# Blockwise causal attention and a gated MLP on one core: Q and K loads of four heads, a third xq buffer, and a looser rule for early fillers

## The chip, the cores and the metric

The kernel runs on one core of a Trainium2 chip. The metric is device time in microseconds of one execution. TensorE is written PE, VectorE DVE, ScalarE ACT, GpSimd POOL and SyncE SP, as the profile does.

## The reference

There are 8 batches of 8 heads, 576 positions and 64 values per head. Attention is causal by blocks of 64 positions; its output, 4608 rows of 512, goes through a two-layer network with a gate.

```
scores = q @ k.T / sqrt(64);  masked where block(row) < block(column), block = position // 64
attn   = exp(scores - max) / sum;   x = (attn @ v) as [4608, 512]
h = x @ w_in                       # [512, 2048]
g = h / (1 + exp(-beta * h))
out = g @ w_out                    # [2048, 512], float32
```

## The kernel before

**Units.** Attention works in 32 units of one batch and two heads (`u = 4 * b + c`). In a unit PE multiplies Q and K (L692; repeats with held weights appear as L434), ACT takes the exponential of 1024 columns at a time into `E` (L706, and L718 for the last 64), DVE clears the masked blocks with memsets (L712, L714), PE multiplies by V with a column of ones added for the sums (L744, 30 matmuls for five query tiles and two heads), and DVE takes the reciprocal (L756) and writes the normalised output to `xq` (L763), a tile of bf16 of which there are two. `xq` is then turned into `xT`: by PE and a copy in batches 0 to 2 (L783, L791 or L793), by a DMA transpose that SP issues in batches 3 to 7 (L770, `XB = 3`). A unit's P·V takes an `xq` slot when it is placed, and the slot is free again when its transpose has read it.

**Loading Q and K.** In batches 0 and 1 each unit loads its own two heads of Q and of K (L606), casts them (L613, POOL or DVE), and PE turns them (L622) into `QKT` through a DVE copy (L630). From batch 2 on (`QB = 2`) one load takes all eight heads of Q, another all eight of K (L641), each into one of two staging tiles `ST` of 128 x 36 x 64 float32 (the slots of class `S8`; the six small parts `ST6` of batches 0 and 1 are cut from the same memory). POOL casts them per two heads into `QKn` (L653, eight casts a batch), and one DMA transpose for two units makes `QKT` (L660). V comes in six loads a batch (L536, L539), and POOL casts it per two heads (L562).

**MLP.** Its rows are cut into nine chunks of 512. For each, PE makes 16 tiles of h (L955), ACT a tanh (L965), and DVE the gated product `gT` (L969). Chunk 0 is multiplied by `w_out` plainly (L991); chunks 1 to 8 use a seven-product scheme for 2 x 2 blocks with sums made on DVE (L852, products L885, evacuation L900 and L903). Weights are loaded by POOL's queue (L490 for `w_in`, L495 for `w_out`).

**What sets the order.** A planner, `Plan.schedule`, simulates five engines, two DMA rings, eight PSUM banks and all buffer slots with durations that are written into the kernel. It gives each engine a fixed list of instructions, and semaphore waits follow from the dependencies. Engines then work through their lists in order. Where a tile takes a slot or a bank, its users are made to depend on the last users of that slot or bank.

Loads of Q, K and V are chained in one order (`seq`, each with `after` the one before), and those behind the first 30 are lazy: they are placed only when the planner has less than 3 us of transfers left in SP's ring. In the order, V of a batch follows the loads of Q and K of unit `4 * b + 1` (from batch 2 on).

**Fillers.** Up to 400 small matmuls with no use for the result (L511 in whole form, L513 as a pair on two halves of the array) are offered to the planner at the lowest priority until 50 us of its time. One is placed where PE has nothing else and enough of banks 4 to 7 are free:

```
if o.fill and (now > o.fill or sum(k >= 4 for k in banks) < 3):
    continue
```

A filler takes one of these banks for 110 ns of the plan, and like every user it waits for the bank's last users.

Of the kernel before, what the change touches and what calls it, by code (L numbers as in the profile page):

```python
# [7 lines left out]
bf16 = mybir.dt.bfloat16  # L8
# [3 lines left out]
NPAIR = 4  # L12
# [36 lines left out]
class Plan:  # L49
# [8 lines left out]
    FIRST, LAND0, BOTH0 = 14000.0, 2150, .8  # L58
    BACKLOG = 3000.0
    RING = 6000.0  # L60

    def __init__(self):
        self.ops = []
# [19 lines left out]
    def schedule(self):  # L83
        free = {c: list(range(n)) for c, n in self.classes.items()}
        last = {(c, i): [] for c, n in self.classes.items() for i in range(n)}
        banks = list(range(8))
# [15 lines left out]
        now, nsched = 0.0, 0  # L102
# [66 lines left out]
        while nsched < len(self.ops) - len(fill) or pend or rings["H"] or rings["S"] or late:  # L169
            if not events:  # L170
                raise RuntimeError("the plan has no way on")
            now = heapq.heappop(events)
            flow(now)
            while pend and pend[0][0] <= now + 1e-9:
                _, _, o = heapq.heappop(pend)
# [20 lines left out]
            while progress:  # L196
                progress = False
                for e in engs:
# [4 lines left out]
                    for o in pool:  # L203
                        if e not in o.engs:
                            continue
                        if o.ready + o.rest + slack > now + 1e-9:
                            heapq.heappush(events, o.ready + o.rest + slack)
                            continue
                        if o.after is not None and o.after.start is None:
                            continue  # L210
                        if o.lazy and left["H"] > self.BACKLOG:
                            continue
                        if o.fill and (now > o.fill or sum(k >= 4 for k in banks) < 3):
                            continue
                        if not can(o):
                            continue
                        if len(o.engs) > 1:
                            other = [x for x in o.engs if x != e]
                            if any(eng_free[x] <= now and len([1 for q in pool if x in q.engs and q.ready <= now]) <
                                   len([1 for q in pool if e in q.engs and q.ready <= now]) for x in other):  # L220
                                continue
                        if o.fill:
                            o.mode = mode or "full"
                        k = (o.prio, o.idx) if e in ("PE",) else (o.prio, o.ready, o.idx)
                        if e == "PE" and mode is not None and o.mode != mode:
                            k = (o.prio + 0.25, o.idx)
                        if best is None or k < best[0]:
                            best = (k, o)
                    if best is None:
                        continue  # L230
                    o = best[1]
                    pool.remove(o)
                    for t in o.tiles:
                        if t.slot is None:
                            if t.cls == "PP":
                                a = next(a for a in t.at if a in banks and a + 1 in banks)
# [24 lines left out]
                    if o.dma is not None:  # L261
                        x = "S" if e == "POOL" else "H"
# [92 lines left out]
def bass_blockwise_causal_attn__then__act_swish_beta_kernel(  # L355
# [10 lines left out]
    with es:  # L366
        def sb(name, shape, dt):
            return es.enter_context(nc.sbuf_tensor(name, shape, dt))

        NQ = 2  # L370
        QB, XB, CAST = 2, 3, "POOL"
        NE = 3
        PARTS = [((0, 4, "SP", range(6)), (4, 8, "SP", range(2)), (4, 8, "POOL", range(2, 6)))] + [((0, 8, "SP", range(6)),)] * 7
        GROUPS = [((0,), (1,), (2,), (3,))] + [((0, 1), (2, 3))] * 7
        NS = 6
# [2 lines left out]
        RX = 5 * RC  # L378
        OV = sb("OV", [128, 5120], f32)
        ST = [sb(f"ST{i}", [128, 36, 64], f32) for i in range(2)]  # L380
        ST6 = [s[0:96].rearrange("p t d -> p (t d)")[:, 768 * i:768 * i + 768].rearrange("p (h j d) -> p h j d", h=2, j=6)
               for s in ST for i in range(3)]
        Vs = [sb("Vs0", [128, 5, 8, 64], f32), OV[:, 2560:5120].rearrange("p (t h d) -> p t h d", t=5, h=8)]
# [3 lines left out]
        QKn = [sb(f"QKn{i}", [128, 2, 2, 768], bf16) for i in range(NQ)]  # L387
        Vn = [sb(f"Vn{i}", [128, 5, 8, 66], bf16) for i in range(NQ)]
        QKT = [sb(f"QKT{i}", [128, 2, 2, 640], bf16) for i in range(3)]
# [4 lines left out]
        E3 = [e[:, 0:3072].rearrange("p (c h n) -> p c h n", c=3, h=2) for e in Ef]  # L394
        E4 = [e[:, 3072:3136] for e in Ef]
        inv = [sb(f"inv{i}", [128, 10], f32) for i in range(3)]
        xq = [sb(f"xq{i}", [128, 5, 128], bf16) for i in range(2)]
        xT = sb("xT", [128, 4, RX], bf16)
        identF = sb("identF", [128, 128], f32)
        identB = sb("identB", [128, 128], bf16)  # L400
# [10 lines left out]
        identW = identF[:].bitcast(bf16)  # L411
        NFILL, TFILL = 400, 50000.0
        P = Plan()
        for c, n in (("ST", NS), ("QKn", NQ), ("V", NQ), ("Vs", NQ), ("QKT", 3), ("E", NE), ("EX", 1), ("inv", 3), ("xq", 2),
                     ("th", 3), ("gT", 2), ("ost", NO), ("S2", 1), ("S3", 1)):
            P.slots(c, n)
        P.slots("S8", 2)

        def mm(n):
            return max(n / 2.4 + 3, 55.0)  # L420
# [50 lines left out]
        for i in range(NQ, NE + 1):  # L471
# [4 lines left out]
                  xfer=100, dma=("d_beta", 1), prio=0.1)  # L476
# [107 lines left out]
            return [z for z in ((0, n, x0), (n, 5 - n, 0)) if z[1]]  # L584

        xt = []
        whole, early6 = {}, []
        QKI, QKX = 1000, 5400
        for u in range(NU):
            b, c = divmod(u, NPAIR)  # L590
            Tv = tl[b]
            p = c % 2
# [5 lines left out]
            if b < QB:  # L598

                turned = []  # L600
                for w, (nm, src) in enumerate((("Q", q), ("K", k))):
                    ts, pt = P.tile("ST"), P.tile("P1")
                    early6.append(ts)

                    def fl(g, e, ts=ts, src=src, b=b, c=c):
                        return [g.dma_start(ST6[ts.slot].rearrange("p h j d -> p h (j d)"),  # L606
                                            src[b, 2 * c:2 * c + 2].rearrange("h (p j) d -> p h (j d)", j=6))]

                    o = ld[nm, u] = P.op("SP", 420, fl, tiles=[ts], xfer=1170, prio=u, dma=["d_S", 0, 1])
                    o.pkt = 80.0  # L610

                    def fn(g, e, ts=ts, tn=tn, p=p, w=w):
                        return g.tensor_copy(QKn[tn.slot][0:96, p, w, :].rearrange("p (j h d) -> p j h d", j=6, h=2),  # L613
                                             ST6[ts.slot].rearrange("p h j d -> p j h d"))

                    onp = u not in (0, 3) or w == 1
                    o = P.op("POOL" if onp else "DVE", 850 if onp else 750, fn, deps=[o], tiles=[ts, tn],
                             prio=-40 + 3 * u if onp else -1)

                    def ft(g, e, tn=tn, pt=pt, p=p, w=w):  # L620
                        for i in range(6):
                            z = g.transpose(PSb[:, pt.slot, 96 * i:96 * i + 96],  # L622
                                            QKn[tn.slot][0:96, p, w, 128 * i:128 * i + 128], identB[0:96, 0:96])
                        return z

                    o = P.op("PE", 6 * 43, ft, deps=[o, c4], tiles=[tn, pt, tt_], lat=6 * 43 + 170, mode="full",
                             prio=pr(u))

                    def fc(g, e, pt=pt, td=tt_, p=p, w=w):
                        return g.tensor_copy(QKT[td.slot][:, p, w, 0:576].rearrange("c (p j) -> c p j", j=6),  # L630
                                             PSb[:, pt.slot, 0:576].rearrange("c (j p) -> c p j", j=6))

                    turned.append(P.op("DVE", dve_t(576), fc, deps=[o], tiles=[pt, tt_], prio=-5))
            elif p == 0:

                for w, (nm, src) in enumerate((("Q", q), ("K", k))):
                    if c == 0:
                        ts = whole[w] = P.tile("S8")

                        def fl(g, e, ts=ts, src=src, b=b):  # L640
                            return [g.dma_start(ST[ts.slot][:], src[b].rearrange("h t d -> (h t) d").rearrange(  # L641
                                "(i p) d -> p i d", p=128))]

                        o = P.op("SP", QKI, fl, deps=[o for t in early6 for o in t.users] if b == QB else [],
                                 tiles=[ts], xfer=QKX, prio=u, dma=["d_S8", 0, 1])
                        for i in range(NPAIR):
                            ld[nm, u + i] = o
                    ts, o = whole[w], ld[nm, u]
                    for a in range(2):
                        def fn(g, e, ts=ts, tn=tn, a=a, w=w, c=c):  # L650
                            x = ST[ts.slot][:, 9 * (c + a):9 * (c + a) + 5, :]
                            x = bass.AP(x.tensor, x.offset, [x.ap[0], [64, 5], [256, 2], [1, 64]])
                            return g.tensor_copy(  # L653
                                QKn[tn.slot][:].rearrange("p a w n -> p (a w n)")[:, 640 * (2 * a + w):][:, 0:640]
                                .rearrange("p (t h d) -> p t h d", t=5, h=2), x)

                        casts.append(P.op(CAST, 740, fn, deps=[o], tiles=[ts, tn], prio=u))

                def ft(g, e, tn=tn, td=tt_):
                    return [g.dma_start_transpose(QKT[td.slot][:].rearrange("c a w (t n) -> c (a w t) n", n=128),  # L660
                                                  QKn[tn.slot][:].rearrange("p a w n -> p (a w n)")[:, 0:2560])]

                turned = [P.op("SP", 3250, ft, deps=casts, tiles=[tt_, tn], xfer=3200, prio=-1, dma=["d_T", 0, 1])]
# [421 lines left out]
```

## Time and profile before

| | |
|---|---|
| median of 10 runs | 340.74 us (339.1 to 345.13) |
| profiled execution, its own time | 342.27 us |
| its span, first to last instruction | 340.4 us |
| PE busy, all matmuls | 324.7 us |
| ACT busy | 211.8 us |
| DVE busy | 219.1 us |
| POOL busy | 83.7 us |
| SP's hardware DMA queue | 58.3% of 16 engines' span, 39.14 MB |
| mean granted PE clock | 0.990 |

The page divides the span into 40 slices and gives each engine's busy share as a digit. A line of a wait names the waiting instruction, what released it, the total, the count and the longest. In timelines a row gives the start, the duration, the engine, the line and operation, the output and input, and in square brackets the idle time before it and its releaser. SPq is the queue of DMA instructions on SP: the duration there is that of issuing. Busy times of PE are modelled, so a busy PE is not always a PE at its peak.

### The profile page before, as it was taken

Reading aid. Unit: us, or ns where it says so; the run is one execution under the profiler, and the core shown is the slowest. Engines: PE = TensorE matmul, PEld = TensorE weight load, DVE = VectorE, ACT = ScalarE, POOL = GpSimd, SP = SyncE. Lnnn points to the kernel's source line nnn. Section 1 sums busy time; section 2 is a strip of 40 time slices with the busy share of each in tenths; the row PEclk is TensorE's granted clock in tenths of the full one; section 3 lists DMA queues with packets and bytes.
Section 4 is the critical chain, followed back from the end, with each engine's and each line's share of the span. In section 5 each row is a group of like instructions: output and inputs, shape, how many; then the busy total and the mean of one; then the engine's idle time right before and its main releaser. Section 6 shows DMA issues by size and latency. Waiting matters only on the chain.

```text
span 340.4 us, 7452 instructions
## 1 busy us (share of the span) xinstructions
PE 324.7 (95%) x3104; PEld 205.1 (60%) x3081; DVE 219.1 (64%) x447; ACT 211.8 (62%) x314; POOL 83.7 (25%) x127
## 2 busy tenths in 40 slices
PE   7798999999998999998999998999999999999995
PEld 4376446544686447754665676566656766666684
DVE  4718867479563788447966674667576766666742
ACT  1862994278636886777688736877677545544511
POOL 7675180216414300531044205303000000000000
PEclk9789999999999999999999999999999999999999
DMA  8999899999999595999879999994221211110023
GB/s 217 224 240 232 192 228 237 226 235 220 207 212 203 143 214 113 188 223 188 168 156 209 196 218 230 185 212 113 73 60 24 79 34 33 37 57 31 17 78 123
DMA packets 113313, 53.41 MB, mean 157 GB/s; under 512 B 83568, under 2 KB 112768, under 8 KB 113280
## 3 DMA queue, kind: packets, MB, share of 16 engines
q1 hardware_dynamic: 98432, 39.14, 58.3%
q10 hardware_dynamic: 9280, 9.44, 8.5%
q0 software_dynamic: 5568, 4.36, 8.1%
q8 instruction: 24, 0.39, 0.5%
q14 instruction: 9, 0.07, 0.1%
HBM read 36.71 MB, written 9.44 MB: 136 GB/s over the span
## 4 chain that ended last, share of the span: by engine, by line
PE 79%; ACT 8%; DVE 5%; DMA 4%; issue 2%; POOL 0%; POOLq 0%; ACTq 0%
PE PS L955 30%; PE PS L885 26%; PE PS L744 7%; PE PS L692 7%; DMA xT<-xq 4%; ACT E L706 4%; PE PS L991 4%; ACT th L965 3%; DVE gT L969 2%; PE PS L511 2%; PE PS L513 2%; PE PS L783 1%; PE PS L622 1%; DVE xq L763 1%; DVE QKT L630 1%
## 5 line engine op out<-in xcount | busy, mean ns | idle before, releaser
L955 PE MATMUL PS<-xT,w_in 128*128 128x512 bf16 x543 | 130.8, 379 | 4.1 <-DMA xT<-xq 1.3
L965 ACT ACTIVATE th<-PS,beta 128x512 f32<-128x512 f32 x144 | 96.7, 696 | 60.9 <-PE PS L955 60.3
L969 DVE SCALAR_TENSOR_TENSOR gT<-th,PS 128x512 f16<-128x512 f32 x144 | 95.8, 681 | 38.9 <-ACT th L965 38.1
L706 ACT ACTIVATE E<-PS 128x1024 bf16<-128x1024 f32 x93 | 92.1, 1027 | 32.3 <-PE PS L692 32.2
L955 PEld LDWEIGHTS PS<-xT,w_in 128*128 128x128 bf16 x576 | 53.0, 98 | 57.9 <-issue 2.7
L885 PE MATMUL PS<-w_out,gT 128*128 128x256 f16 x512 | 63.9, 273 | 0.3 <-ACT ost L900 0.3
L885 PEld LDWEIGHTS PS<-w_out,gT 128*128 128x128 f16 x512 | 48.7, 98 | 12.3 <-issue 0.6
L653 POOL CAST QKn<-ST 128x640 bf16<-128x640 f32 x48 | 36.2, 754 | 46.1 <-DMA ST<-in_k_dram 25.8
L562 POOL CAST Vn<-Vs 128x640 bf16<-128x640 f32 (+1 forms) x28 | 21.2, 755 | 94.1 <-DMA Vs<-in_v_dram 92.9
L692 PE MATMUL PS<-QKT 64*64 64x64 bf16 (+4 forms) x328 | 37.7, 302 | 0.4 <-ACT E L706 0.3
L744 PEld LDWEIGHTS PS<-Vn,E 128*128 128x128 bf16 x930 | 31.3, 97 | 7.3 <-DVE E L712 2.4
L744 PE MATMUL PS<-Vn,E 128*128 128x65 bf16 x930 | 32.6, 193 | 2.5 <-DVE E L712 1.2
L885 PE MATMUL PS<-OV 128*128 128x256 f16 x256 | 32.1, 273 | 0.0
L900 ACT ACTIVATE ost<-PS 128x512 f32<-128x512 f32 x32 | 19.2, 600 | 20.6 <-PE PS L885 20.2
L692 PEld LDWEIGHTS PS<-QKT 64*128 64x128 bf16 (+1 forms) x328 | 13.6, 96 | 26.6 <-issue 13.9
L885 PEld LDWEIGHTS PS<-OV 128*128 128x128 f16 x256 | 24.3, 98 | 5.8 <-issue 0.4
L763 DVE TENSOR_TENSOR xq<-PS,inv 128x640 bf16<-128x640 f32 x32 | 26.2, 820 | 0.7
L903 DVE SCALAR_TENSOR_TENSOR ost<-PS,ost 128x512 f32<-128x512 f32 x24 | 16.4, 688 | 13.4 <-PE PS L885 8.7
L712 DVE MEMSET E<- 64x64 uint32 x62 | 6.9, 112 | 26.3 <-ACT E L706 24.5
L852 DVE TENSOR_TENSOR OV<-gT 128x1024 f16<-128x1024 f16 x32 | 22.1, 703 | 0.4
L885 PE MATMUL PS<-OV,gT 128*128 128x256 f16 x128 | 15.9, 273 | 0.0
L991 PE MATMUL PS<-w_out,gT 128*128 128x512 f16 x64 | 15.2, 380 | 0.0
(60 smaller groups left out, 172.9 us busy)
## 6 DMA issues: line engine op xcount, KB each, us to landing
out_dram<-ost ACTq DMA_DIRECT2D x36, 256.0 KB, 2.8
Vs<-in_v_dram SPq DMA_DIRECT2D x24, 256.0 KB, 5.0
ST<-in_q_dram SPq DMA_DIRECT2D x8, 288.0 KB, 6.4
ST<-in_k_dram SPq DMA_DIRECT2D x8, 288.0 KB, 6.6
w_in<-in_moe_w_in_dram POOLq DMA_DIRECT2D x4, 512.0 KB, 10.3
w_out<-in_moe_w_out_dram POOLq DMA_DIRECT2D x4, 512.0 KB, 11.6
OV<-in_v_dram SPq DMA_DIRECT2D x4, 256.0 KB, 10.3
Vs<-in_v_dram SPq DMA_DIRECT2D x6, 128.0 KB, 7.9
```

The lines of the kernel that those rows point to most:

```text
L562: return g.tensor_copy(Vn[t.slot][:, 0:n, g0:g1, 0:64], Vs[ts.slot][:, 0:n, g0:g1, :])
L653: return g.tensor_copy(QKn[tn.slot][:].rearrange("p a w n -> p (a w n)")[:, 640 * (2 * a + w):][:, 0:640] .rearrange("p (t h d) -> p t h d ...
L692: z = g.matmul(o, QKT[tqk.slot][r, p, 1, 128 * t + y:128 * t + m + y], x)
L706: return g.activation(E3[es_(te)][:, g0, :, :], PS[:, ps.slot:ps.slot + 2, :], ACT.Exp, scale=0.125)
L744: z = g.matmul(o, eblk(te, t, i, h), Vn[Tv.slot][:, t, 2 * c + h, 0:65], start=(t == 0), stop=(t == i))
L763: return g.tensor_tensor(xq[tx.slot][:].rearrange("p i (h d) -> p h i d", h=2), both(pv, 0, 64), x, ALU.mult)
L852: return P.op("DVE", dve_t(SZ * HC / 2), mk(lambda g: g.tensor_tensor(fo(), fx(), fy(), op)), deps=deps, tiles=tiles, prio=prio)
L885: x = g.matmul(PS[:, ps.slot, HM * w:HM * w + HM], fa()[:, j, 128 * w:128 * w + 128], fb()[:, j, :], start=first and w == 0 and j == 0, st ...
L955: z = g.matmul(PS[:, ph.slot, :], w_in[:, c, 128 * j:128 * j + 128], xT[:, c, row % RX:row % RX + RC], start=(c == 0), stop=(c == 3))
L965: return g.activation(th[tt.slot][:], PS[:, ph.slot, :], ACT.Tanh, scale=beta[:, j:j + 1])
L969: return g.scalar_tensor_tensor(out=gT[tg.slot][:, j, :], in0=th[tt.slot][:], scalar=1.0, in1=PS[:, ph.slot, :], op0=ALU.add, op1=ALU.mult)
L991: z = g.matmul(PS[:, po.slot, 0:d1 - d0], gT[tg.slot][:, j, 128 * w:128 * w + 128], w_out[:, j, d0:d1], start=(j == 0), stop=(j == NJ - 1))
```

## The change

There are three parts. Fillers that are planned before 24 us need one free bank of 4 to 7 instead of three; later ones need three as before. From batch 2 on, a load brings four heads of Q or K (two units) instead of eight, into one of four half tiles `STh` that are cut from the same two staging tiles; with it the planner's figures for such a load are halved (issue 1000 to 550 ns, transfer 5400 to 2700 ns), and because the loads of Q and K are now those of units `4 * b` and `4 * b + 2`, V of a batch stands in the load order between the first and the second pair. There are three `xq` buffers instead of two.

```diff
--- before.py
+++ after.py
@@ -58,6 +58,7 @@
     FIRST, LAND0, BOTH0 = 14000.0, 2150, .8
     BACKLOG = 3000.0
     RING = 6000.0
+    EARLY = 24000.0
 
     def __init__(self):
         self.ops = []
@@ -210,7 +211,7 @@
                             continue
                         if o.lazy and left["H"] > self.BACKLOG:
                             continue
-                        if o.fill and (now > o.fill or sum(k >= 4 for k in banks) < 3):
+                        if o.fill and (now > o.fill or sum(k >= 4 for k in banks) < (3 if now > self.EARLY else 1)):
                             continue
                         if not can(o):
                             continue
@@ -378,6 +379,7 @@
         RX = 5 * RC
         OV = sb("OV", [128, 5120], f32)
         ST = [sb(f"ST{i}", [128, 36, 64], f32) for i in range(2)]
+        STh = [s[:, 18 * i:18 * i + 18] for s in ST for i in range(2)]
         ST6 = [s[0:96].rearrange("p t d -> p (t d)")[:, 768 * i:768 * i + 768].rearrange("p (h j d) -> p h j d", h=2, j=6)
                for s in ST for i in range(3)]
         Vs = [sb("Vs0", [128, 5, 8, 64], f32), OV[:, 2560:5120].rearrange("p (t h d) -> p t h d", t=5, h=8)]
@@ -394,7 +396,7 @@
         E3 = [e[:, 0:3072].rearrange("p (c h n) -> p c h n", c=3, h=2) for e in Ef]
         E4 = [e[:, 3072:3136] for e in Ef]
         inv = [sb(f"inv{i}", [128, 10], f32) for i in range(3)]
-        xq = [sb(f"xq{i}", [128, 5, 128], bf16) for i in range(2)]
+        xq = [sb(f"xq{i}", [128, 5, 128], bf16) for i in range(3)]
         xT = sb("xT", [128, 4, RX], bf16)
         identF = sb("identF", [128, 128], f32)
         identB = sb("identB", [128, 128], bf16)
@@ -411,10 +413,10 @@
         identW = identF[:].bitcast(bf16)
         NFILL, TFILL = 400, 50000.0
         P = Plan()
-        for c, n in (("ST", NS), ("QKn", NQ), ("V", NQ), ("Vs", NQ), ("QKT", 3), ("E", NE), ("EX", 1), ("inv", 3), ("xq", 2),
+        for c, n in (("ST", NS), ("QKn", NQ), ("V", NQ), ("Vs", NQ), ("QKT", 3), ("E", NE), ("EX", 1), ("inv", 3), ("xq", 3),
                      ("th", 3), ("gT", 2), ("ost", NO), ("S2", 1), ("S3", 1)):
             P.slots(c, n)
-        P.slots("S8", 2)
+        P.slots("S4", 4)
 
         def mm(n):
             return max(n / 2.4 + 3, 55.0)
@@ -584,8 +586,8 @@
             return [z for z in ((0, n, x0), (n, 5 - n, 0)) if z[1]]
 
         xt = []
-        whole, early6 = {}, []
-        QKI, QKX = 1000, 5400
+        early6 = []
+        QKI, QKX = 550, 2700
         for u in range(NU):
             b, c = divmod(u, NPAIR)
             Tv = tl[b]
@@ -634,21 +636,19 @@
             elif p == 0:
 
                 for w, (nm, src) in enumerate((("Q", q), ("K", k))):
-                    if c == 0:
-                        ts = whole[w] = P.tile("S8")
-
-                        def fl(g, e, ts=ts, src=src, b=b):
-                            return [g.dma_start(ST[ts.slot][:], src[b].rearrange("h t d -> (h t) d").rearrange(
-                                "(i p) d -> p i d", p=128))]
-
-                        o = P.op("SP", QKI, fl, deps=[o for t in early6 for o in t.users] if b == QB else [],
-                                 tiles=[ts], xfer=QKX, prio=u, dma=["d_S8", 0, 1])
-                        for i in range(NPAIR):
-                            ld[nm, u + i] = o
-                    ts, o = whole[w], ld[nm, u]
+                    ts = P.tile("S4")
+
+                    def fl(g, e, ts=ts, src=src, b=b, c=c):
+                        return [g.dma_start(STh[ts.slot], src[b, 2 * c:2 * c + 4].rearrange("h t d -> (h t) d").rearrange(
+                            "(i p) d -> p i d", p=128))]
+
+                    o = P.op("SP", QKI, fl, deps=[o for t in early6 for o in t.users] if b == QB else [],
+                             tiles=[ts], xfer=QKX, prio=u, dma=["d_S4", 0, 1])
+                    for i in range(2):
+                        ld[nm, u + i] = o
                     for a in range(2):
-                        def fn(g, e, ts=ts, tn=tn, a=a, w=w, c=c):
-                            x = ST[ts.slot][:, 9 * (c + a):9 * (c + a) + 5, :]
+                        def fn(g, e, ts=ts, tn=tn, a=a, w=w):
+                            x = STh[ts.slot][:, 9 * a:9 * a + 5, :]
                             x = bass.AP(x.tensor, x.offset, [x.ap[0], [64, 5], [256, 2], [1, 64]])
                             return g.tensor_copy(
                                 QKn[tn.slot][:].rearrange("p a w n -> p (a w n)")[:, 640 * (2 * a + w):][:, 0:640]
```

## The prediction

> **What bounds the kernel now.** I read the page's engine totals and 40 slices first, because they say whether there is anything to win and where.
>
> ```profile
> PE 324.7 (95%) x3104; PEld 205.1 (60%) x3081; DVE 219.1 (64%) x447; ACT 211.8 (62%) x314; POOL 83.7 (25%) x127
> PE   7798999999998999998999998999999999999995
> PEclk9789999999999999999999999999999999999999
> ```
>
> TensorE (PE) sets the time: 324.7 of 340.4 us busy. It is idle for 15.7 us in all, and from slice 6 on (after 43 us) it is hardly ever below nine tenths. The one other weakness is the clock row: 7 and 8 in the second and third slice, so between 8.5 and 25 us. The table by stages of 1 us shows that stretch (columns: window, its length, then busy us and instructions of PE, PEld, DVE, ACT, POOL; granted clock; DMA share; GB/s).
>
> ```profile
> 9.00:10.00 1.00, 0.86 (x17) 0.50 (x15) 0.79 (x2) 1.00 (x2) 0.83 (x2) 1.00 1.08 266
> 10.00:11.00 1.00, 0.33 (x7) 0.18 (x5) 0.90 (x3) 1.00 (x3) 1.00 (x2) 1.00 1.17 228
> 12.00:13.00 1.00, 0.71 (x12) 0.23 (x9) 0.97 (x2) 1.00 (x3) 1.00 (x2) 1.00 1.22 197
> 13.00:14.00 1.00, 0.28 (x6) 0.13 (x3) 1.00 (x2) 1.00 (x2) 0.94 (x2) 0.66 1.21 222
> 14.00:15.00 1.00, 0.99 (x8) 0.45 (x7) 0.90 (x3) 0.66 (x1) 0.00 (x0) 0.50 1.52 240
> 19.00:20.00 1.00, 1.00 (x12) 0.72 (x10) 0.00 (x0) 0.72 (x1) 0.94 (x2) 0.50 1.12 248
> 20.00:21.00 1.00, 1.00 (x16) 0.55 (x12) 0.17 (x1) 0.47 (x2) 0.31 (x2) 0.92 1.08 234
> ```
>
> PE has holes from 9.9 to 13.9 us; at 13.3 us the clock falls to 0.50 and is back at about 20.1 us. So for 6.8 us every matmul takes twice as long, and about 3.4 us of PE work is lost. Next the PE timeline, for what PE waited on before the fall:
>
> ```profile
> 10.93 0.39 PE L511 MATMUL PS<-identF,identB 128*128 128x256 bf16 x2 [0.67 <-DVE QKT L630]
> 13.88 0.66 PE L622 MATMUL PS<-identB,QKn 96*128 96x96 bf16 x6 [0.72 <-DVE QKn L613]
> ```
>
> L511 is a filler: it itself waits 0.67 us, for the VectorE copy that last read its bank. The second line is a real wait: a cast on VectorE that took 1.70 us. Then the waits of PE between 40 and 320 us (total us, times, longest):
>
> ```profile
> PE PS L955 <- DMA xT<-xq: 1.3, 1, 1.3
> PE PS L744 <- DVE E L712: 1.2, 1, 1.2
> PE PS L744 <- DVE gT L969: 0.8, 1, 0.8
> PE PS L744 <- DMA xT<-xq: 0.4, 1, 0.4
> PE PS L885 <- ACT ost L900: 0.3, 1, 0.3
> ```
>
> With two waits of 0.2 these are 4.4 us, all that a better order can win after 40 us. For the first of them, the timeline around it:
>
> ```profile
> 201.39 0.73 SPq L641 DMA_DIRECT2D ST<-in_q_dram  x1
> 202.16 6.84 SPq L770 DMA_TRANSPOSE xT<-xq  x1
> 209.45 0.73 SPq L641 DMA_DIRECT2D ST<-in_k_dram  x1
> 211.87 1.67 PE L955 MATMUL PS<-xT,w_in 128*128 128x512 bf16 x7 [1.27 <-DMA xT<-xq]
> ```
>
> The transpose is issued behind a load of eight heads (1.18 MB) and sits 6.84 us in SP's queue; the chain of waits books 9.44 us for it (202.16 to 211.60), and PE stands 1.27 us.
>
> **The change, part by part.** Sums are made on the profiled execution: 342.27 us, of which 340.40 are the span and 1.87 lie around it. It is 1.53 above the median of 340.74, so I carry differences over to the median.
>
> *Early fillers.* No real work is added or taken away; up to 24 us of the plan, a filler may go where one bank from 4 to 7 is free instead of three. A filler of two matmuls costs some 0.13 us at full clock (16 in 1.06 us at 20.73). In PE's holes it costs nothing: the hole covers it. Without that cover 20 more would cost 20 x 0.13 = 2.6 us. If they hold the clock, the real PE work between 13.3 and 20.1 us (L622 at 13.88 and 15.81, L692 at 15.08, 16.41, 18.22 and 18.63: 0.66 + 0.66 + 0.80 + 0.61 + 0.26 + 0.61 = 3.6 us) takes half, which is 1.8 us. Is that on the path? ScalarE's exponentials run from 8.42 to 24.38 us and stand for PE in this stretch 0.73 + 0.32 + 0.44 + 0.53 + 0.53 + 0.29 = 2.8 us, so yes, it can take up 1.8. The P·V matmuls of units 0 and 1 start at 24.02, while their V casts end at 20.07 (18.57 + 1.50): there is room of 4 us. What is late next is POOL: batch 1's casts start at 23.83 behind the weight loads' issue and end at 29.24, and DMA engines are at 1.05 to 1.5 of their share all the while; these do not move with PE's clock. The first MoE matmul (L955, 32.38) comes 8.4 us after P·V begins, and I let it move with P·V. The bounds are 3.4 us (all of the lost clock) and a loss of 2.6; I take the gain of 1.8, nearest to the ScalarE row.
>
> The clock row shows that holes adding up to 1.8 us in 5 (9 to 14 us: 0.86 + 0.33 + 1.00 + 0.71 + 0.28 busy) are enough to lose it, and that it came back only after some 6 us of nearly full PE. The Trainium skill ("TensorE: Matmul & The Clock Gate", Part 1) says that the clock halves after an idle window of about 3.4 us and returns after one busy window. Read so, these short holes should not have cost the clock at all and fillers would win 0 us; the trace decides here.
>
> *Loads of four heads.* From batch 2 on, 12 loads become 24 of half the size, on the same bytes, packets of 256 B and 48 casts (722 ns median each). Each added issue costs SP 0.73 us and about 0.37 for setting its shape: 12 x 1.1 = 13.2 us more of SP in 180 us, on an engine that mostly waits. The order changes too: Q and K of the second half now go after the six V loads of the batch, so V (issues of 0.58 us where nothing blocks) moves ahead of 1.18 MB, and both the QKT transposes (two per batch, 3.7 us each in SP's queue) and the xT transposes meet loads half as long. The first half of Q and K lands after 1.18 MB rather than 2.36. At the place shown, the load's data came 8.6 us after its issue (cast at 210.05); half of that is 4.3, so the transpose lands near 207.3, ahead of the matmul that now waits from 210.6. The wait of 1.27 us goes. What follows is L692 at 213.48, behind L955 in PE's order. The waits on E and gT (1.2 and 0.8) come from how far QK is placed ahead of P·V; the new order can remove both (2.0) or add as many. The nearest row for an added one is again the 1.27: of 24 xT transposes one misses now. I take zero for these.
>
> A 1.18 MB load lands in 8.6 us here (median), and traffic runs at 190 to 250 GB/s with 256 B packets in either version, so I take no loss of bandwidth. The Trainium skill ("DMA: Bandwidth & Descriptors", Rules for kernel authors) speaks against the change: it asks for at least 1 MiB per DMA and for merging small transfers, and its fit puts about 2 us of fixed time on a DMA of GpSimd's path. Were that paid in series, 12 more loads would be an estimated 24 us of queue time; this trace has no row for it.
>
> *Third xq.* It adds no instruction. At 195.03 P·V waited 0.36 us on a DMA transpose that had to release its xq; with a third buffer it starts as soon as its E is there (memset at 194.05), so 0.36 goes. Bounds: 0.36, and nothing lost but what order brings.
>
> Sum: 1.8 + 1.27 + 0.36 = 3.4 us. 342.27 - 3.4 = 338.9 for a profiled execution like this one, 340.74 - 3.4 = **337.3 us** for the median.
>
> **Rivals.** *The clock is not held, or holding it is worth nothing* (0.20). For it: the filler at 10.93 stood 0.67 us itself, the 1.70 us cast before 13.88 stays, and loads and POOL fix 23.83. Against: of the 66 fillers in the trace (32 L511, 34 pairs of L513) those from 16.94 on did bring the clock back. Only 1.27 + 0.36 = 1.6 us remain: 339.1 us, within half a per cent.
>
> *SP's queue becomes the late one* (0.24), slower. In each of batches 2 to 7 two more issues, 2.2 us, stand before the transposes, and the planner's list of due times is off by that. If one transpose in each batch makes PE wait as at 211.87 for 1.1 us, that is 6.6 us lost; less 3.4 it is 3.2 slower, 343.9 us. It decides from about five such waits (5.1 us = 3.4 + 1.7). For it: load issues block for 4.3 us at the median when the ring is full (5.7 at most), and now there are four per batch. Against: only one of 24 misses now, and each block should be half as long.
>
> **How the numbers follow.** Forecast 0.56 (337.3), clock rival 0.20 (339.1), queue rival 0.24 (343.9). A measurement of this kernel tells some 0.5% (1.7 us) from no change, so these are also the chances of faster, same and slower. The low end: all of the clock, 3.4, and all waits after 40 us, 4.4, give 7.8, so 332.9. The high end is the queue rival's 343.9. The likeliest case alone runs from 332.9 to 339.0.
>
> **What would show it.** Right: granted clock 1.0 from 13 to 20 us with more L511 and L513 matmuls before 24 us; ScalarE's last exponential of batch 0 near 22.6 instead of 24.4; first L955 near 30.6 instead of 32.4; no wait of PE on xT above 0.5 us; 24 load issues on L641's successor. Wrong: clock still 0.50 around 15 us; more filler time but L955 no earlier; or PE waits on xT or QKT that add up to more than 4.4 us after 40 us.

## The result and the profile after

The changed kernel takes 338.7 us (median of 15 runs, 338.3 to 341.6). Measured alongside, the kernel before took 342.64 us (52 runs, 338.9 to 347.1). Runs more than 1.5% above the fastest of their kernel are left out of ratios, which is why the ratio is nearer to 1 than those two medians: it is 0.9934, 95% interval 0.9906 to 0.9962, so 2.3 us faster (1.3 to 3.2). I had forecast 3.4 us from 340.74 (ratio 0.990). The profiled execution went from 342.27 to 338.46 us and its span from 340.4 to 336.7. Those differences, 3.8 and 3.7 us, are near my sum of 3.4, and that is misleading: the runs below show that two of its three terms bring nothing that can be seen, and that the third is about twice its size.

The page after, the rows of section 1 and 2 for PE and its clock:

```profile
PE 325.2 (97%) x3126; PEld 206.1 (61%) x3106; DVE 224.7 (67%) x447; ACT 211.7 (63%) x314; POOL 87.2 (26%) x127
PE   7998999999999999999999999999999999999995
PEclk9999999999999999999999999999999999999999
```

The clock row has no 7 and 8 any more, and PE is idle for 11.5 us of the span (336.7 - 325.2) instead of 15.7. By stages of 1 us the early stretch reads (same columns as before):

```profile
10.00:11.00 1.00, 1.00 (x18) 0.76 (x18) 0.66 (x1) 1.00 (x2) 0.79 (x3) 1.00 1.16 230
13.00:14.00 1.00, 1.00 (x18) 0.71 (x20) 0.89 (x3) 1.00 (x3) 1.00 (x3) 1.00 1.22 227
19.00:20.00 1.00, 1.00 (x18) 0.77 (x18) 0.17 (x1) 0.93 (x2) 0.94 (x2) 1.00 1.09 226
```

PE is full and at clock 1.00 where it was 0.33 full at 10 us and at half clock at 19 us. The first MoE matmul is at 30.83 us (before 32.38; I had said 30.6). PE's waits from 40 to 320 us:

```profile
PE PS L955 <- issue: 0.8, 5, 0.2
PE PS L692 <- DVE xq L763: 0.3, 1, 0.3
PE PS L783 <- ACT E L718: 0.3, 1, 0.3
```

Three waits of 0.2 us follow, 2.0 in all where there were 4.4. No wait on a DMA transpose is left, and no single one is longer than 0.3 us. ScalarE's last exponential of batch 0 ends at 22.97 us (I had said 22.6), and 124 filler matmuls start before 24 us where there were 98. So everything that I had named as a sign of being right is in this one trace, if only roughly for ScalarE.

### The profile page after: what moved, and what is told of

It reads as the page before. It is cut to its first block, busy times and chain, and to the rows that moved or that the text cites. A ratio compares the mean times of both kernels' runs of the same rounds, so it can differ in the third digit from the quotient of the medians.

```text
span 336.7 us, 7498 instructions
## 1 busy us (share of the span) xinstructions
PE 325.2 (97%) x3126; PEld 206.1 (61%) x3106; DVE 224.7 (67%) x447; ACT 211.7 (63%) x314; POOL 87.2 (26%) x127
## 4 chain that ended last, share of the span: by engine, by line
PE 84%; ACT 7%; DVE 5%; issue 2%; ACTq 0%; POOL 0%; POOLq 0%
PE PS L955 31%; PE PS L885 28%; PE PS L744 8%; PE PS L692 7%; PE PS L991 4%; ACT E L706 4%; DVE gT L969 3%; PE PS L513 2%; ACT th L965 2%; PE PS L515 2%; PE PS L783 1%; PE PS L624 1%; DVE OV L852 1%; DVE gT L852 1%; DVE xq L763 0%
## 5 line engine op out<-in xcount | busy, mean ns | idle before, releaser
L955 PE MATMUL PS<-xT,w_in 128*128 128x512 bf16 x540 | 130.1, 379 | 3.5 <-issue 0.8
L955 PEld LDWEIGHTS PS<-xT,w_in 128*128 128x128 bf16 x576 | 52.7, 98 | 56.8 <-issue 3.2
L885 PE MATMUL PS<-w_out,gT 128*128 128x256 f16 x512 | 63.2, 273 | 0.0
L653 POOL CAST QKn<-ST 128x640 bf16<-128x640 f32 x48 | 39.1, 816 | 23.7 <-DMA ST<-in_q_dram 10.7
L692 PE MATMUL PS<-QKT 64*128 64x192 bf16 (+4 forms) x328 | 37.1, 297 | 0.3 <-DVE xq L763 0.3
L692 PEld LDWEIGHTS PS<-QKT 64*128 64x128 bf16 (+1 forms) x328 | 13.4, 95 | 27.0 <-issue 15.4
L852 DVE TENSOR_TENSOR OV<-gT 128x1024 f16<-128x1024 f16 x32 | 23.7, 750 | 0.5
```

The source lines that it names most:

```text
L653: return g.tensor_copy(QKn[tn.slot][:].rearrange("p a w n -> p (a w n)")[:, 640 * (2 * a + w):][:, 0:640] .rearrange("p (t h d) -> p t h d ...
L692: z = g.matmul(o, QKT[tqk.slot][r, p, 1, 128 * t + y:128 * t + m + y], x)
L852: return P.op("DVE", dve_t(SZ * HC / 2), mk(lambda g: g.tensor_tensor(fo(), fx(), fy(), op)), deps=deps, tiles=tiles, prio=prio)
L885: x = g.matmul(PS[:, ps.slot, HM * w:HM * w + HM], fa()[:, j, 128 * w:128 * w + 128], fb()[:, j, :], start=first and w == 0 and j == 0, st ...
L955: z = g.matmul(PS[:, ph.slot, :], w_in[:, c, 128 * j:128 * j + 128], xT[:, c, row % RX:row % RX + RC], start=(c == 0), stop=(c == 3))
```

## The experiments

**The parts by themselves.** Four kernels: the filler rule alone, the loads alone, the third xq alone, and loads with xq but the old filler rule.

```diff
-  sum(k >= 4 for k in banks) < 3
+  sum(k >= 4 for k in banks) < (3 if now > self.EARLY else 1)      # e1_fill: this alone on the kernel before
   # e2_loads: STh, S4, loads of four heads alone;  e3_xq: xq 2 -> 3 alone
   # e4_loads_xq: the changed kernel with "< 3" again
```

Filler rule alone: 

> The kernel before with the early filler rule alone. Theory of the clock: the granted clock stays at 1.0 from 13 to 20 us, first L955 at 30.8 us instead of 32.4, and the whole gain is made there: 1.6 to 1.8 us faster (ratio 0.995), nothing won after 40 us. Rival, the order as a whole: a shift of 1.6 us at the start changes what meets what later, so the time may fall by anything from 0 to 4 us and PE's waits after 40 us change from 4.4 us.

Loads alone: 

> The kernel before with the loads of four heads alone. By the prediction's sum: the wait of 1.27 us on xT goes and nothing else, 1.3 us faster, first L955 still at 32.4 us with the clock at half from 13 to 20 us. By the trace after, in which PE's idle time after 40 us fell by some 2.5 us: 2 to 2.5 us faster. Rival, SP's queue is late: slower by 1 us or more, with waits of PE on DMA transposes.

Third xq alone: 

> The kernel before with the third xq alone. By the sum: 0.36 us faster, no more, since one wait of P.V on a transpose goes. Rival, the order: another slot lets the planner put P.V elsewhere from the first units on, and the time moves by 1 us or more in either direction.

Loads and xq: 

> The changed kernel with the old filler rule (three free banks at all times). If the parts add: 1.6 us faster by the prediction's terms (1.27 + 0.36), 2.5 by the trace after, and slower than the changed kernel by the fillers' 1.6 to 1.8. If they don't add, it differs from the sum of the runs with loads alone and xq alone by more than 1 us.

Ratios to the kernel before: fillers alone 1.010 (1.005 to 1.015), **slower** by some 3.4 us; loads alone 0.9925 (0.990 to 0.995); xq alone 1.002 (0.998 to 1.007); loads and xq 0.995 (0.992 to 0.998). The part that I gave the largest share of the gain costs time when it is alone, and the loads alone are as fast as the whole change.

Each execution lists its mean granted clock, which shows what is mixed in these medians. I count the clock as held at 0.9975 or more; no run of these kernels lies between 0.996 and 0.998.

| kernel | runs with the clock held, their median us | runs where it fell, their median us |
|---|---|---|
| before (86 runs beside the experiments) | 51, 340.6 | 35, 344.0 |
| fillers alone | 2, 341.4 | 10, 345.9 |
| xq alone | 2, 338.5 | 10, 343.1 |
| loads alone | 10, 337.3 | 2, 339.7 |
| loads and xq | 9, 337.4 | 3, 341.0 |
| all three (the change) | 13, 338.6 | 3, 341.4 |

Read down the middle column: loads take 3.3 us away (340.6 to 337.3), xq adds 0.1, fillers add 1.2 (337.4 to 338.6). This last step compares runs of different rounds. The fastest run of the kernel before was the same in both (338.87 and 338.89), which speaks for the 1.2; but the ratios, each to the kernel before of its own round, do not show it (0.995 without the fillers, 0.9934 with them). Either way no gain from the fillers can be told from noise. Nor do they visibly lower the number of falls: 3 of 12 runs without, 3 of 16 with them. Two rows of the middle column rest on two runs each.

**Where the fillers cost.** In the trace after, the timeline at the first turns (PE):

```profile
6.39 1.40 PE L513 MATMUL PS<-identF,identB 128*128 128x256 bf16 x6
7.63 0.42 PE L624 MATMUL PS<-identB,QKn 96*128 96x96 bf16 x6
...
9.18 0.76 PE L692 MATMUL PS<-QKT 64*128 64x512 bf16 x8
```

and in the trace of loads alone, which has the old rule and happened to hold the clock:

```profile
6.39 0.66 PE L624 MATMUL PS<-identB,QKn 96*128 96x96 bf16 x6
...
8.84 0.75 PE L692 MATMUL PS<-QKT 64*128 64x512 bf16 x8
...
29.87 0.81 PE L955 MATMUL PS<-xT,w_in 128*128 128x512 bf16 x3 [0.34 <-ACT xT L791]
```

Six fillers of 0.23 us each stand ahead of the turn of K, which starts at 7.63 instead of 6.39, though its input was ready (POOL's cast ended at 6.03). By the first multiplication of Q and K only 0.34 us of that is left (9.18 for 8.84); by the first P·V it is 1.0 again (22.50 for 21.51), so fillers behind it cost the larger part.

The first L955 sums it up. With the new rule it is at 30.83 to 31.17 us in three traces, all with the clock held until then. With the old rule it is at 28.74 to 30.62 in five traces that held the clock and at 31.48 to 33.55 in four that had lost it (the other kernels of this section are among them). So the new rule is an insurance: it costs 0.2 to 2.4 us in an execution where the clock holds anyway and saves 0.3 to 2.7 where it would have fallen.

I then let the one-bank rule start only at 8 us of the plan:

```diff
-  (3 if now > self.EARLY else 1)
+  (1 if 8000.0 < now <= self.EARLY else 3)
```

> The changed kernel, but the one-bank rule holds only from 8 to 24 us of the plan (three banks before 8 us and after 24). The runs so far: with loads and xq but without the fillers 337.6 us, with them 338.7. Theory, the cost is fillers that stand ahead of real work: in the trace after, six of them (1.40 us) sit at 6.39 us before the first turn of K, which starts at 7.63 instead of 6.39. Without these the first QK is at about 8.8 instead of 9.18, first L955 at 29.6 to 30.2 instead of 30.8, and the median 337.5 to 338.0. Rival, the cost is the later fillers or the order: 338.7 as in the changed kernel.

Measured 339.3 us, ratio 0.993 (0.990 to 0.996). With the clock held (6 of 12 runs) it is 338.0, between 338.6 and 337.4. But the clock fell in the other 6; in the trace it was at half from 31.4 to 34.8 us. There the first multiplication of Q and K comes at 8.45, earlier still than without the rule, and yet P·V starts at 22.46, as with all fillers (22.50), and the first L955 at 31.79, not at 30. The median is a miss, and the claim that only those six fillers cost is wrong.

**What in the loads is worth 3 us.** Three kernels take the loads apart: loads of two heads; whole loads whose DMA alone is cut in two, with the planner's order untouched; and four heads with V behind both halves as before.

```diff
   # e6_two_heads: eight quarter parts of ST, one load per unit and operand
   # e7_split_dma, on the kernel before:
-  return [g.dma_start(ST[ts.slot][:], src[b]...)]
+  return [g.dma_start(ST[ts.slot][:, 18 * z:18 * z + 18, :], src[b, 4 * z:4 * z + 4]...) for z in range(2)]
   # e8_v_last, on e2_loads:
-  if u == 4 * b + (3 if b < 2 else 1):
+  if u == 4 * b + 3:
```

> The kernel before with loads of two heads instead of eight from batch 2 on (eight quarter parts of staging, the planner's figures 300 and 1350 ns), old fillers and two xq. Theory, what counts is how much is in front of a transpose in SP's queue: the longest time of an xT transpose to landing goes from 11.5 (eight heads) over 7.6 (four heads) to 5 or 6 us, and the time stays at the 337.5 of loads of four heads or gains up to 0.7. Rival, SP's queue: 24 further issues of about 0.6 us in front of transposes make it slower than 337.5 by 1 us or more.

> The kernel before with each load of eight heads issued as two DMAs of four heads one after the other, on one semaphore, the plan and the order of all engines left as they are. Theory, the gain needs the second half to be released and ordered apart: no change, 0 within 1 us, longest xT landing still above 10 us. Rival, the size of a DMA itself is what matters: 2 us or more faster.

> Loads of four heads alone (old fillers, two xq), with V of a batch behind both halves of Q and K in the order of loads, as in the kernel before, instead of between them. Theory, what counts is that a load in front of a transpose is half as long: 337 to 338 us, as with loads alone (337.5). Rival, the gain comes from V's earlier place or from an order that happened to fit: 339.5 us or more.

Here my theory fell. The kernel before with nothing changed but the DMA cut in two takes 337.2 us, ratio 0.9895 (0.984 to 0.995), which is the whole gain and the lowest ratio of all, though from 6 runs and with an interval that overlaps the others. I had expected none. PE's list of instructions is the same in both. Two heads: 0.993 (0.989 to 0.997), 337.9 with the clock held, so no more than four. V last: 0.995 (0.991 to 0.999), 338.2 with the clock held in 8 of 12 runs, which leaves a worth of up to 1 us to V's earlier place but does not show it (those runs reach from 337.0 to 342.1).

Is it the size of the DMA or its form? In the kernel before, the answer for the load's line (SP: name, count, ns min/median/max) has an instruction that no smaller load has, and the longest landing of an xT transpose is 11.5 us:

```profile
L641 SPq MOVE_SHAPE ST<-in_q_dram x6: 368/374/383, 39.1 to 201.0; - x6
L641 SPq DMA_DIRECT2D ST<-in_q_dram x6: 726/726/751, 39.5 to 201.4; - x6
L641 SPq DMA_DIRECT2D ST<-in_k_dram x6: 730/4328/5725, 40.7 to 209.5; - x6
...
L770 SPq DMA_TRANSPOSE xT<-xq x24: 1200/1274/7528, 116.0 to 266.8; - x24
DMA to landing us min/median/max: 2.4/3.4/11.5
```

The packets differ too. The pages, before and then after:

```profile
DMA packets 113313, 53.41 MB, mean 157 GB/s; under 512 B 83568, under 2 KB 112768, under 8 KB 113280
```

```profile
DMA packets 154977, 53.41 MB, mean 159 GB/s; under 512 B 139056, under 2 KB 154432, under 8 KB 154944
```

Between 512 B and 2 KB before has 29,200 and after 15,376. The difference is 13,824, or 1152 for each of 12 loads of 1.18 MB, which is 1 KB a packet. So a load of 36 rows per partition goes out in another form than one of 18. Two more cuts with the plan unchanged tell form from size, 28 rows with 8, and four times nine:

```diff
+  return [g.dma_start(ST[ts.slot][:, y:z, :], x[:, y:z, :]) for y, z in ((0, 28), (28, 36))]   # e9; e10: 0, 9, 18, 27, 36
```

> As the run with each load of eight heads split in two DMAs with the plan unchanged (337.2 us), but split unevenly: 28 of the 36 rows per partition (0.92 MB) and 8 (0.26 MB). The whole load goes out in packets of about 1 KB after a MOVE_SHAPE instruction, the halves in packets of 256 B without one. Theory of the form: what hurts is the form of the whole load; if the part of 28 is issued without MOVE_SHAPE, the whole gain comes, 336.5 to 338 us. Rival, the size of the largest DMA: 0.92 MB is near 1.18, so at most half of the gain, 338.5 us or more with the clock held.

> The same with four DMAs of nine rows (0.29 MB each), one semaphore, plan unchanged. Theory of the form: no more than two halves give, 336.5 to 338 us. Theory of the size: another 1 us or more. Theory of SP's queue: 24 more issues of some 0.6 us in front of transposes, slower than 338.

28 and 8 rows: 337.45 us, ratio 0.990 (0.987 to 0.994), 337.3 with the clock held; four times nine: 0.992 (0.988 to 0.996), 337.0 with the clock held. (These two ran on another chip, with their own runs of the kernel before.) A DMA of 0.92 MB is as good as one of 0.29. The trace of 28 and 8 has no MOVE_SHAPE, and a longest xT landing of 6.9 us:

```profile
L642 SPq DMA_DIRECT2D ST<-in_q_dram x12: 584/1808/4161, 39.9 to 195.3; - x12
...
L770 SPq DMA_TRANSPOSE xT<-xq x24: 1200/1274/3222, 113.5 to 261.1; - x24
DMA to landing us min/median/max: 2.4/3.5/6.9
```

**How the form costs PE time.** The fillers alone, once more, for a trace of one of their long executions:

> The early filler rule alone once more, for a trace (its runs were 341.2 to 350.2 us, and 10 of 12 had a mean clock below 0.998). Theory: the clock is held until 30 us by the fillers, and is lost later, between 100 and 220 us, in a hole of PE of over 2 us behind an xT transpose that stands behind a load of eight heads, as in the trace of the run with xq alone (2.62 us at 206.8). Rival: it is lost early in spite of the fillers.

It took 346.5 us. The clock is 1.00 until 211.5 us. The timeline at the place that the prediction showed (SP's queue, then PE):

```profile
201.28 0.73 SPq L642 DMA_DIRECT2D ST<-in_q_dram  x1
202.06 7.67 SPq L771 DMA_TRANSPOSE xT<-xq  x1
210.17 0.72 SPq L642 DMA_DIRECT2D ST<-in_k_dram  x1
```

```profile
208.50 1.08 PE L745 MATMUL PS<-Vn,E 128*128 128x65 bf16 x30
213.15 3.19 PE L956 MATMUL PS<-xT,w_in 128*128 128x512 bf16 x7 [3.57 <-DMA xT<-xq]
```

and the stages there (PE busy is the second number, the clock the third from the end):

```profile
210.00:212.00 2.00, 0.00 (x0) 0.00 (x0) 0.86 (x2) 0.00 (x0) 1.30 (x2) 0.88 1.21 134
212.00:214.00 2.00, 0.85 (x2) 0.44 (x4) 0.00 (x0) 0.00 (x0) 1.58 (x3) 0.50 0.99 232
214.00:216.00 2.00, 2.00 (x6) 0.61 (x4) 0.61 (x1) 0.69 (x1) 0.00 (x0) 0.50 1.11 218
216.00:218.00 2.00, 2.00 (x9) 0.54 (x7) 0.77 (x2) 1.34 (x2) 0.00 (x0) 0.50 1.22 216
```

PE stands 3.57 us for xT, and from 211.5 until 218.3 the clock is at half. The wait that was 1.27 us in the trace of before is here long enough to cost the clock a second time. The run with xq alone shows the same with a wait of 2.62 us that ends at 209.4, and clock 0.50 from 209 to 212. This is also where the fillers' slowness alone comes from in this trace: they kept the clock early, and it was lost here. It is one execution. In the first trace of the same kernel (341.87 us) the wait on xT is 1.2 us and the clock holds until 330 us. That a PE which is earlier leaves the transposes less room, and so 10 of 12 runs lost the clock, fits this but was not tried by itself; with xq alone, which has no added fillers, it was 10 of 12 as well. In the trace of 28 and 8 rows the same transpose gets through SP's queue in 2.49 us:

```profile
194.67 4.82 SPq L642 DMA_DIRECT2D ST<-in_q_dram  x2
199.53 2.49 SPq L770 DMA_TRANSPOSE xT<-xq  x1
202.07 4.96 SPq L642 DMA_DIRECT2D ST<-in_k_dram  x2
```

and L955 starts at 206.22 without a wait. From the start of the load's issue to the end of the transpose's issue it is 8.4 us in the long execution (201.28 to 209.73) and 7.4 here (194.67 to 202.02), only 1.1 apart. What is different is that SP is ahead of PE. With the cut in two halves, SP's first xT transpose comes 3.6 us earlier than before (112.39 for 116.02) and this load 7.4 us earlier (193.97 for 201.39), while PE gains 3.6 us at the first L955 (28.74 for 32.38) and 4.9 at L692 of this place (198.98 for 203.86). SP wins some 2.5 us on PE in between. Part of it is one place: from K's load to the end of the transpose behind it, 11.9 us before (173.63 to 185.52) and 9.8 with the cut (169.14 to 178.92).

PE's waits from 40 to 320 us in the trace of the halves:

```profile
PE PS L744 <- DVE E L712: 1.2, 1, 1.2
PE PS L885 <- ACT ost L900: 0.3, 1, 0.3
```

Three waits of 0.2 follow, 2.1 in all. Of the waits before, those on xT (1.3), on gT (0.8) and on xq (0.4) are gone, and the wait on E stays. This matches the time from the first L955 to the end, in which the early clock has no part:

| trace | first L955, us | from there to the end of the span, us |
|---|---|---|
| before (whole loads) | 32.38 | 308.0 |
| fillers alone, twice (whole loads) | 31.08, 31.17 | 309.0, 313.5 |
| xq alone (whole loads) | 29.61 | 309.7 |
| two halves, plan unchanged | 28.74 | 305.6 |
| 28 and 8 rows, plan unchanged | 29.20 | 305.6 |
| four times nine, plan unchanged | 33.42 | 306.1 |
| loads alone; with V last | 29.87; 30.62 | 305.3; 306.3 |
| loads of two heads | 31.48 | 306.6 |
| loads and xq | 33.55 | 305.7 |
| the change; fillers from 8 us only | 30.83; 31.79 | 305.9; 307.2 |

Every trace with whole loads is at 308.0 or more, every other at 307.2 or less, and the 307.2 has the clock's fall at 31.4 us in it. Between before and the halves it is 2.4 us, which is the three waits.

So this is shown: with plan and order unchanged, cutting the load takes away PE's waits on xT, gT and xq, and in two executions with whole loads a late xT cost PE its clock on top. No trace of the kernel before has the clock held, so how its 340.6 us are made up is not shown. That the form is what hurts is the reading that fits all cut kernels, and 28 and 8 rows speak against size. But a cut load is also two DMAs or more where there was one. Whether it is MOVE_SHAPE, the packets of 1 KB or the single DMA that holds up what stands behind it is open: no run had one without the others.

**A better version.** The kernel before with each load cut in two (337.2) beats the changed kernel (338.7). Against the kernel before they stand at 0.9895 and 0.9934, with intervals that overlap; with the clock held its 5 runs lie at 336.1 to 337.9 and the changed kernel's 13 at 338.3 to 340.0, so they do not meet, though they were not measured in the same rounds. The halves with the other two parts of the change were not tried.

## Why the prediction was right and wrong

*What bounds the kernel:* right. PE is at 97% after, and the time went where its idle time and its clock went.

*Early fillers, a gain of 1.8 us:* this is the step that failed. In the profile the mechanism is as I described it: the clock stays at 1.00, and L955 moves by 1.55 us. But alone on the kernel before, fillers made it 1.0% slower, and on top of loads and xq they bring no gain that can be seen. The term was taken from one execution that had lost the clock at 13 us, and I carried it over to the median of a kernel that holds its clock in 51 of 86 runs. The hint was in my own text: the profiled execution lay 1.53 us above the median. In the other runs the fillers cost what I had set to zero with the words "the hole covers it": some of them have no hole, and with the clock held the term measured +1.2 us (across rounds), between my bounds of -3.4 and +2.6. A smaller slip: the 1.8 us of holes that I called enough to lose the clock reach past its fall at 13.3; up to there they add to some 1.3.

*Loads of four heads, a gain of 1.27 us:* right in the place, about half the size. They give 2.6 us as a ratio (1.7 to 3.4) and 3.3 with the clock held. The waits on gT and xq, for which I took zero here, go with the wait on xT, which makes 2.4 in the traces. And I priced the wait on xT as one execution showed it; in two others, of kernels with whole loads, it is 2.6 and 3.6 us, with the clock at half behind it. The cause was not the one I gave, either. I wrote that the loads are half as long and that packets are 256 B in either version. They are not: before's were 1 KB, and a load of 0.92 MB in 256 B packets brings the whole gain.

On the rule that the Trainium skill gives against the change ("DMA: Bandwidth & Descriptors", Rules for kernel authors: at least 1 MiB per DMA for the highest bandwidth, and merge small ones), the measurement decides: cutting 1.18 MB into 2 x 0.59 with the plan unchanged is 1.05% faster (0.5 to 1.6), and the mean rate in the profile goes from 157 to 160 GB/s.

*Added issues of 1.1 us each:* too dear. A load of four heads takes 0.57 to 0.61 us to issue where nothing blocks, and sets no shape. Behind another load it takes 2.3 us at the median (K in the trace after) where it was 4.3; that a full ring is the reason, as I wrote, is not shown.

*Third xq, 0.36 us:* nothing measurable, +0.1 us with the clock held (337.3 to 337.4) and ratio 1.002 alone. The wait of 0.36 us that it was to take away is gone with the loads alone, so beside them the term was counted twice.

*Rivals.* The clock rival had half of the truth: fillers are worth nothing in the median. It erred on why: in all three traces with the full rule the clock is held until the first L955. SP's queue as the late one did not come; the longest xT landing fell from 11.5 to 6.2 us.

## What to carry to other kernels

A difference that you price from one profiled execution is a difference of that execution: before it goes to a median, ask whether the stall is in the other runs too, by the spread of the times and the clock of each. Work that fills a hole is free only if the hole is there when it runs; in an in-order queue it stands in front of real work in all other executions. When a large load delays what is queued behind it, cut its DMA before changing the order of anything, and look whether instruction and packets keep their form.

## What the runs showed of the hardware

A load of 128 partitions x 36 rows of 256 B was issued with a MOVE_SHAPE instruction (0.37 us) and in packets of 1 KB; the same load in parts of 28, 18 or 9 rows had neither, and the xT transposes landed within 6.1 to 9.2 us at the longest, where with whole loads it was 10.6 to 11.5. In a hole of PE of 3.57 us late in the kernel the clock fell to half for some 6.8 us (211.5 to 218.3), in one of 2.62 us for some 3.4 (209.0 to 212.4). The fall came some 1.9 and 2.2 us after PE's last matmul before the hole. Whether one and the same program loses its clock differs from run to run: 35 of 86 runs of the kernel before did. The clock row reads 1.00 from the start, and yet in the trace after the same filler took 0.23 us at 6.39 (6 in 1.40) and 0.12 at 7.89 (11 in 1.36), so the row does not show how slow PE is in its first microseconds.
